# Attention's first tiles: V of batch 0 asked for behind the first q tile, the gate's load moved into ScalarE's program, tile 0's products ahead of the turns of tile 1's q

## The chip, the cores and the metric

The kernel runs on one core of one Trainium2 chip. Its time is the device time of one launch in microseconds (us). Before the change three runs took 647.5, 648.42 and 651.75 us; the median is 648.42 us.

## The reference

The program chains three layers. Only the first is touched by the change, but everything later depends on it.

```
# q, k, v: 4 batches x 8 heads x 576 rows x 64
k_p = k.reshape(B, H, 72, 8, D).mean(axis=3)        # keys pooled by eight
v_p = v.reshape(B, H, 72, 8, D).mean(axis=3)        # values pooled by eight
attn = softmax(q @ k_p.T / sqrt(D));  out = attn @ v_p
x = out.transpose(0, 2, 1, 3).reshape(2304, 512)
logits = x @ w_gate                                  # 8 experts, the best one per token
x = gate_weight * (relu(x @ w1[expert]) @ w2[expert])   # with a capacity per expert
h = x @ w_in;  g = s * relu(h)**2 + b;  y = g @ w_out
```

## The kernel before, in words

Attention is cut into 20 tiles: four batches b, and in each five blocks of 128 rows (the fifth has 64). `load_k`, `load_v` and `load_q` (lines 124 to 137 and 207 to 212) ask for K, V and q from HBM; all of these DMAs stand in the queue of SyncE (SP), in program order, so a load that waits holds back all that follow. K of a batch comes in two DMAs of 576 KB, V in six (576 KB, 448 KB and four of 32 KB), q of a tile in one of 256 KB. K is in pieces of 2 KB, V too, q in pieces of 256 bytes. `load_gate` (lines 116 to 121) asks for the gate's weights `wg` in five small DMAs, and these stand in the program of ScalarE (ACT).

The DMAs of SP and ACT share eight completion counters, named DMAHW0 to DMAHW7 in the order below, which are handed out in turn. A DMA that gets a counter waits until the DMA that had it before has landed. So every load waits for the one eight places ahead of it, whichever queue that was in. Apart from that, a load waits until its buffer is free: q has four buffers, `vraw` has one.

For one tile the work is: `turn_q` transposes q on TensorE (PE) and ACT copies it to `qT` (lines 214 to 222); `products` multiplies it with the pooled keys `kbd` (line 230); `maxima` and `weights` take the row maximum and the difference on VectorE (DVE, lines 236 and 242) and the exponentials on ACT (lines 246 and 247); `turn_e` transposes the exponentials on PE and ACT copies them (lines 259 to 266); `values` multiplies them with `vx` (lines 275 and 277), and DVE divides. `vx` holds the pooled values and, beside them, the pooled values times the gate's weights. `pool_all` sums eight rows to one in three steps, split between DVE and GpSimd (POOL); `prep_v0` turns the pooled values on PE (line 186), copies them and fills `vx`; `prep_v1` multiplies them with `wg` on PE (line 200) and needs all five gate DMAs.

Each engine works in program order. The order of the first tiles is written out by hand, ahead of the loop over the tiles (lines 444 to 482); the change is there. PSUM has one buffer for each of the names `tq`, `te`, `sc`, `o` and `misc`.

Of the kernel before, what the change touches and what calls it, by code (L numbers as in the profile page):

```python
# [72 lines left out]
def rows(t):  # L73
    return P if t < NB - 1 else S - (NB - 1) * P


def attention(nc, tc, c, a, cap, capp, left, big, xd, run, hist, first, ps0):
# [3 lines left out]
    with ExitStack() as es:  # L81
# [34 lines left out]
        def load_gate():  # L116
            wv = a["moe_w_gate"].rearrange("(c q w d) e -> c q d w e", c=2, q=2, w=2)
            for i in range(4):
                ci, q = divmod(i, 2)
                nc.scalar.dma_start(out=wg[D * q:D * q + D, ci, 2 * q:2 * q + 2], in_=wv[ci, q])  # L120
            nc.scalar.dma_start(out=wg[D:P, 2], in_=a["moe_w_gate"].rearrange("(p w d) e -> w d p e", w=2, d=D)[1])
# [3 lines left out]
        def load_k(b):  # L125
            r = big.tile([SP, H, POOL, D], F32, name="kraw")
            src = a["k"][b].rearrange("h (n j) d -> n h j d", j=POOL)
            for i in range(2):
                nc.sync.dma_start(out=r[:, 4 * i:4 * i + 4], in_=src[:, 4 * i:4 * i + 4])
            raw["k", b] = r  # L130

        def load_v(b):
            src = a["v"][b].rearrange("(p w) (n j) d -> w n p j d", w=2, j=POOL)
            nc.sync.dma_start(out=vraw[0:SP, 0:4], in_=src[0])
            nc.sync.dma_start(out=vraw[SP:P, 0:4], in_=src[1, 0:P - SP])
            for p in range(4):
                nc.sync.dma_start(out=vraw[32 * p + 16:32 * p + 32, 4], in_=src[1, P - SP:, p])
            raw["v", b] = vraw
# [24 lines left out]
        def pool_all(kv, b, h0, h1, eng):  # L163
            for _ in pool_steps(kv, b, h0, h1, eng):
                pass

        def prep_k(b):
            tp = ps0.tile([P, 4, SP], F32, name="misc")
            for p in range(4):
                nc.tensor.transpose(tp[:, p], sums["k", b][:, 2 * p:2 * p + 2].rearrange("n h d -> n (h d)"), c.ident[:SP, :SP])  # L170
            for w in range(2):
                r = slice(D * w, D * w + D)
                dst = kbd[b % 2][r, :, SP * w:SP * w + SP]
                if b:
                    nc.scalar.mul(dst, tp[r], KSCALE)
                else:
                    nc.vector.tensor_scalar(out=dst, in0=tp[r], scalar1=KSCALE, scalar2=None, op0=ALU.mult)
# [19 lines left out]
        def prep_v1(b):  # L197
            tr = ps0.tile([P, G, E], F32, name="misc")
            for p in range(3):
                nc.tensor.matmul(tr[:, 4 * p:4 * p + 4].rearrange("r g e -> r (g e)"), lhsT=vts[b][:, p], rhs=wg[:, p].rearrange("d g e -> d (g e)"), start=True, stop=True)  # L200
            nc.vector.tensor_tensor(out=vx[b % 2][:, :, D + 1:], in0=tr, in1=c.mask.unsqueeze(2).to_broadcast([P, G, E]), op=ALU.mult)
# [5 lines left out]
        def load_q(i):  # L207
            if i < N:
                b, t = tiles[i]
                n = rows(t)  # L210
                qs[i] = two.tile([P, H, D], F32, name="q", bufs=4)
                nc.sync.dma_start(out=qs[i][:n], in_=a["q"][b, :, t * P:t * P + n].rearrange("h s d -> s h d"))

        def turn_q(i, bank="tq"):
            if i < N:
                n = rows(tiles[i][1])
                q = qs.pop(i)
                tq = ps1.tile([P, 2, 4, P], F32, name="te")[:, 0] if bank == "te" else ps0.tile([P, 4, P], F32, name="tq")
                for p in range(4):
                    nc.tensor.transpose(tq[:, p, :n], q[:n, 2 * p:2 * p + 2].rearrange("s h d -> s (h d)"), c.ident[:n, :n])  # L220
                qts[i] = two.tile([P, 4, P], F32, name="qT")
                nc.scalar.copy(qts[i][:, :, :n], tq[:, :, :n])

        def products(i, bank="sc"):
            b, t = tiles[i]
            n = rows(t)
            q = qts.pop(i)
            sc = ps1.tile([P, 2, 512], F32, name=bank)
            for p in range(4):
                nc.tensor.matmul(sc[:n, p // 2, p % 2 * 144:p % 2 * 144 + 144], lhsT=q[:, p, :n], rhs=kbd[b % 2][:, p], start=True, stop=True)  # L230
            return sc

        def maxima(i, sc):
            n = rows(tiles[i][1])
            mx = two.tile([P, 2, 4], F32, name="mx")
            nc.vector.tensor_reduce(out=mx[:n], in_=sc[:n, :, 0:288].rearrange("s j (h k) -> s j h k", k=SP), axis=AX.X, op=ALU.max)
            return mx

        def weights(i, sc, mx):
            n = rows(tiles[i][1])  # L240
            s = two.tile([P, 4, 2 * SP], F32, name="s", bufs=3)
            nc.vector.tensor_tensor(out=s[:n].rearrange("s (j p) (w k) -> s j (p w) k", j=2, w=2), in0=sc[:n, :, 0:288].rearrange("s j (h k) -> s j h k", k=SP),
                                    in1=mx[:n].unsqueeze(3).to_broadcast([n, 2, 4, SP]), op=ALU.subtract)

            e = two.tile([P, 4, 32], F32, name="e", bufs=3)
            nc.scalar.activation(e[:n], s[:n, :, 2 * SP - 32:], AF.Exp)
            nc.scalar.activation(s[:n, :, 0:P], s[:n, :, 0:P], AF.Exp)
            ss[i] = s, e
# [8 lines left out]
        def turn_e(i):  # L257
            if i < N:
                n = rows(tiles[i][1])
                s, e = ss.pop(i)  # L260
                te = ps1.tile([P, 2, 4, P], F32, name="te").rearrange("k j p s -> k (j p) s")
                for p in range(4):
                    nc.tensor.transpose(te[:, p, :n], s[:n, p, 0:P], c.ident[:n, :n])
                nc.tensor.transpose(te[:, 4, :n], e[:n].rearrange("s p k -> s (p k)"), c.ident[:n, :n])
                ets[i] = two.tile([P, NB, P], F32, name="eT", bufs=4)
                nc.scalar.copy(ets[i][:, :, :n], te[:, 0:NB, :n])
# [175 lines left out]
                nc.vector.tensor_copy(lists, n)  # L442

        load_k(0)
        load_gate()
        load_q(0)
        load_q(1)
        load_v(0)
        load_q(2)
        load_q(3)  # L450
        load_k(1)
# [6 lines left out]
        o = ps1.tile([P, 2, 512], F32, name="o")  # L458
# [1 line left out]
            nc.tensor.transpose(o[:, 0, 0:P], c.ident, c.ident)  # L460
        turn_q(0)
        prep_k(0)
        turn_q(1, "te")
        sc = products(0, "o"), products(1)
        pool_all("v", 0, 0, 2, nc.gpsimd)
        weights(0, sc[0], maxima(0, sc[0]))
        pool_all("v", 0, 2, NB, nc.vector)
        mx = maxima(1, sc[1])
        turn_e(0)
        prep_v0(0)  # L470
        turn_q(2)
        weights(1, sc[1], mx)
        prep_v1(0)
        turn_q(3)
        scores(2)
# [68 lines left out]
        while todo or tails or scales:  # L544
            more = 7
            while more and (todo or tails):
                more -= 1
                if step():
# [4 lines left out]
                    o = ps1.tile([P, 2, 512], F32, name="o")  # L553
# [1094 lines left out]
```

## Time and profile before

| what | value |
|---|---|
| median of three runs | 648.42 us |
| the profiled execution | 649.79 us |
| its span, first to last instruction | 648.1 us |
| PE busy in the span | 588.7 us (91%) |
| DVE, POOL, ACT busy | 367.0, 267.8, 249.9 us |
| mean granted TensorE clock | 0.959 of 2.4 GHz |

The difference of 1.7 us between the profiled execution and its span lies around the program. The profiled execution is 1.4 us above the median, and inside the three runs shown. A row of the timeline gives the start, the duration and, in brackets, how long the engine had been idle and what ended that. The queue rows (SPq, ACTq) show how long the queue was occupied by issuing a DMA, not the transfer itself.

### The profile page before, as it was taken

How to read it: one execution, taken by the hardware profiler on the slowest of the kernel's cores; microseconds unless marked ns; L12 is line 12 of the kernel's file. 1: busy time of each engine (PE TensorE's matmuls, PEld its weight loads, DVE VectorE, ACT ScalarE, POOL GpSimd, SP SyncE). 2: the span in 40 equal slices, each digit the busy share in tenths (PEclk: the TensorE clock that was granted, in tenths of full speed). 3: DMA queues.
4: the chain of work that ended last, by engine and by line, in shares of the span. 5: the costliest groups of instructions: out<-in, count | busy, mean ns of one | idle time of the engine just before them, and what ended most of it. 6: DMA issues, size and time to landing. Idle time of an engine off the chain costs nothing. (4 is left out here: it accounts for less than half of the span.)

```text
span 648.1 us, 11186 instructions
## 1 busy us (share of the span) xinstructions
PE 588.7 (91%) x4005; PEld 545.1 (84%) x4005; DVE 367.0 (57%) x893; ACT 249.9 (39%) x614; POOL 267.8 (41%) x384
## 2 busy tenths in 40 slices
PE   5887988799899979998887899999999999999894
PEld 5787877689799969997887889899899898898784
DVE  4687898888969956654499996424122021120140
ACT  1354554546356635533327425125034042141130
POOL 6557634627165717013234402216435054153381
PEclk8799999799899979999998799999999999999898
DMA  8999776637649884856565101135200101000000
GB/s 164 190 190 182 157 228 182 220 117 261 230 148 307 267 299 126 281 172 214 188 208 231 34 30 37 32 118 209 81 18 6 46 17 33 32 3 17 20 2 20
DMA packets 67950, 86.11 MB, mean 133 GB/s; under 512 B 24713, under 2 KB 40073, under 8 KB 67856
## 3 DMA queue, kind: packets, MB, share of 16 engines
q1 hardware_dynamic: 57168, 71.04, 37.2%
q10 hardware_dynamic: 8240, 7.14, 3.8%
q0 software_dynamic: 2448, 6.82, 3.3%
q8 instruction: 42, 0.69, 0.5%
q14 instruction: 52, 0.43, 0.2%
HBM read 68.09 MB, written 17.58 MB: 132 GB/s over the span
## 5 line engine op out<-in xcount | busy, mean ns | idle before, releaser
L1440 POOL TENSOR_TENSOR gl<-rt,gh 128x256 fp32r<-128x256 f32 (+1 forms) x96 | 71.3, 747 | 99.3 <-ACT gh L1439 57.9
L1445 PE MATMUL bank<-wo,gh 128*128 128x512 f32 (+1 forms) x340 | 99.2, 376 | 0.0
L1113 PE MATMUL bank<-hs,w2h 128*128 128x288 f32 (+1 forms) x308 | 68.9, 312 | 5.0 <-issue 4.6
L936 POOL TENSOR_TENSOR w1l<-kraw,w1h 128x128 fp32r<-128x128 f32 x96 | 51.9, 572 | 51.1 <-ACT w1h L929 51.1
L1445 PEld LDWEIGHTS bank<-wo,gh 128*128 128x128 f32 x340 | 62.0, 188 | 12.2
L1445 PE MATMUL bank<-wo,gl 128*128 128x512 f32 (+1 forms) x170 | 63.8, 375 | 0.0
L1452 DVE SCALAR_TENSOR_TENSOR raw<-bank,sb,c_u 128x512 f32<-128x512 f32 (+1 forms) x14 | 9.9, 710 | 86.9 <-PE bank L1445 86.9
L1113 PEld LDWEIGHTS bank<-hs,w2h 128*128 128x128 f32 x308 | 51.0, 193 | 6.0 <-issue 5.4
L1424 ACT ACTIVATE rt<-tq 128x256 f32<-128x256 f32 (+1 forms) x26 | 9.5, 367 | 113.8 <-PE tq L1040 91.1
L1113 PE MATMUL bank<-hs,w2l 128*128 128x288 f32 (+1 forms) x148 | 45.0, 304 | 0.0
L1425 DVE SCALAR_TENSOR_TENSOR rt<-bank,rt 128x256 f32<-128x256 f32 (+1 forms) x53 | 21.3, 401 | 37.6 <-ACT rt L1424 37.2
L944 POOL DMA_INDIRECT xg<-xd,u_idx x23 | 26.1, 1136 | 34.4 <-DVE r L290 15.3
L1439 ACT CAST gh<-rt 128x256 fp32r<-128x256 f32 (+1 forms) x96 | 36.6, 381 | 7.9 <-DVE rt L1425 7.9
L1453 POOL DMA_INDIRECT out_dram<-raw,it x12 | 11.9, 994 | 64.3 <-DVE raw L1452 63.8
L1445 PEld LDWEIGHTS bank<-wo,gl 128*128 128x128 f32 x170 | 31.9, 188 | 6.5
L1424 ACT ACTIVATE rt<-bank 128x256 f32<-128x256 f32 (+1 forms) x60 | 22.2, 369 | 33.7 <-PE bank L1040 26.5
L230 PE MATMUL sc<-kbd,qT 128*128 128x144 f32 (+1 forms) x152 | 25.5, 317 | 6.2 <-DVE rmine L380 3.6
L1425 DVE SCALAR_TENSOR_TENSOR rt<-tq,rt 128x256 f32<-128x256 f32 (+1 forms) x24 | 9.6, 399 | 35.5 <-ACT rt L1424 35.5
L967 PE MATMUL bank<-xs,w1h 128*128 128x288 f32 (+1 forms) x120 | 27.3, 313 | 2.0 <-DVE hs L970 2.0
L230 PEld LDWEIGHTS sc<-kbd,qT 128*128 128x128 f32 (+1 forms) x152 | 21.9, 201 | 8.4 <-issue 4.9
L1113 PEld LDWEIGHTS bank<-hs,w2l 128*128 128x128 f32 x148 | 28.5, 193 | 0.0
L940 DVE TENSOR_TENSOR w2l<-vraw,w2h 128x512 fp32r<-128x512 f32 x39 | 26.8, 686 | 0.9 <-ACT w2h L939 0.5
(496 smaller groups left out, 1749.4 us busy)
## 6 DMA issues: line engine op xcount, KB each, us to landing
kraw<-in_moe_w_dram SPq DMA_DIRECT2D x14, 1024.0 KB
vraw<-in_moe_w_dram SPq DMA_DIRECT2D x14, 1024.0 KB
c_raw<-in_moe_w_in_dram ACTq DMA_DIRECT2D x13, 512.0 KB
wo<-in_moe_w_out_dram SPq DMA_DIRECT2D x13, 512.0 KB
kraw<-in_k_dram SPq DMA_DIRECT2D x8, 576.0 KB
out_dram<-c_u SPq DMA_DIRECT2D x1, 4608.0 KB
q<-in_q_dram SPq DMA_DIRECT2D x16, 256.0 KB
xd<-xr SPq DMA_DIRECT2D x16, 256.0 KB
```

Source lines behind the costliest of these rows:

```text
L230: nc.tensor.matmul(sc[:n, p // 2, p % 2 * 144:p % 2 * 144 + 144], lhsT=q[:, p, :n], rhs=kbd[b % 2][:, p], start=True, stop=True)
L936: eng.tensor_sub(self.w1l[:, i, z], self.w1(i)[:, z], self.w1h[:, i, z])
L940: eng.tensor_sub(self.w2l[i], self.w2r[:, i], self.w2h[i])
L944: self.nc.gpsimd.indirect_dma_start(out=dst, out_offset=None, in_=self.xd[:have], in_offset=bass.IndirectOffsetOnAxis(ap=idx[:n], axis=0), ...
L967: self.nc.tensor.matmul(p, lhsT=l[:, f, k], rhs=r[k], start=n == 0, stop=n == 3 * KD - 1)
L1113: nc.tensor.matmul(py[d][:, :v.n], lhsT=l[f][:, d * P:d * P + P], rhs=r[f], start=f == 0 and i == 0, stop=f == KF - 1 and i == 2)
L1424: nc.scalar.activation(r, p, AF.Relu)
L1425: nc.vector.scalar_tensor_tensor(out=p if inside else r, in0=p, scalar=0.0, in1=r, op0=ALU.max, op1=ALU.mult)
L1439: nc.scalar.copy(h[:, :n], r)
L1440: (nc.gpsimd if p is None else nc.vector).tensor_sub(l[:, :n], r, h[:, :n])
L1445: nc.tensor.matmul(p[:, c], lhsT=g[:, j * P:j * P + P], rhs=wo[f][:, z, c], start=f == 0 and i == 0, stop=f == KF2 - 1 and i == 2)
L1453: i = nc.gpsimd.indirect_dma_start(out=dst, out_offset=bass.IndirectOffsetOnAxis(ap=ids, axis=0), in_=o[:, c], in_offset=None, bounds_chec ...
```

## The change

Three things are moved in the hand-written start. V of batch 0 is asked for directly behind q of tile 0, ahead of q of tile 1. `load_gate` is called behind the exponentials of tile 0 instead of ahead of everything. And q of tile 1 is turned after the products of tile 0, in the bank `tq` instead of `te`; the products of tile 1 follow it. Nothing is computed differently.

```
         load_k(0)
-        load_gate()
         load_q(0)
+        load_v(0)
         load_q(1)
-        load_v(0)
         load_q(2)
...
         turn_q(0)
         prep_k(0)
-        turn_q(1, "te")
-        sc = products(0, "o"), products(1)
+        sc = products(0, "o")
         pool_all("v", 0, 0, 2, nc.gpsimd)
-        weights(0, sc[0], maxima(0, sc[0]))
+        weights(0, sc, maxima(0, sc))
+        load_gate()
+        turn_q(1)
+        sc = products(1)
         pool_all("v", 0, 2, NB, nc.vector)
-        mx = maxima(1, sc[1])
+        mx = maxima(1, sc)
         turn_e(0)
         prep_v0(0)
         turn_q(2)
-        weights(1, sc[1], mx)
+        weights(1, sc, mx)
```

On ACT the place is its very start. Before, the five gate DMAs are its first instructions:

```order
L120 DMA wg<-in_moe_w_gate_dram 64x2x8 x4
L121 DMA wg<-in_moe_w_gate_dram 64x4x8
L222 ACT_TABLE_LOAD
L222 COPY qT<-tq 128x512
L222 COPY qT<-te 128x512
L246 ACTIVATE e<-s 128x128
L247 ACTIVATE s<-s 128x4x128
L266 COPY eT<-te 128x640
```

And now:

```order
L222 ACT_TABLE_LOAD
L222 COPY qT<-tq 128x512
L246 ACTIVATE e<-s 128x128
L247 ACTIVATE s<-s 128x4x128
L120 DMA wg<-in_moe_w_gate_dram 64x2x8 x4
L121 DMA wg<-in_moe_w_gate_dram 64x4x8
L222 COPY qT<-tq 128x512
L266 COPY eT<-te 128x640
```

The five issues now stand between the exponentials of tile 0 and the copies of tile 1's q and of tile 0's weights. On PE the place is the stretch from the first turn of q to the turn of tile 3's q. Before:

```order
L220 MATMUL tq<-ident,q 128x128 x4
L170 MATMUL misc<-ident,kp 128x72 x4
L220 MATMUL te<-ident,q 128x128 x4
L230 MATMUL o<-kbd_163,qT 128x144 x4
L230 MATMUL sc<-kbd_163,qT 128x144 x4
L263 MATMUL te<-ident,s 128x128 x4
L264 MATMUL te<-ident,e 128x128
L186 MATMUL misc<-ident,vp 128x128 x3
```

And now, from the products of tile 0 on, with the counters that PE waits for:

```order
L230 MATMUL o<-kbd_163,qT 128x144 [waits DVE_49,Activation_49]
L230 MATMUL o<-kbd_163,qT 128x144 x3
L220 MATMUL tq<-ident,q 128x128 [waits DMAHW1_49,PE_49]
L220 MATMUL tq<-ident,q 128x128 x3
L230 MATMUL sc<-kbd_163,qT 128x144 [waits Activation_49]
L230 MATMUL sc<-kbd_163,qT 128x144 x3
L263 MATMUL te<-ident,s 128x128 [waits DVE_49]
...
L200 MATMUL misc<-wg,vT 128x32 [waits DMAHW4_49,DMAHW3_49,DVE_49]
L200 MATMUL misc<-wg,vT 128x32 [waits DMAHW6_49,DMAHW5_49]
L200 MATMUL misc<-wg,vT 128x32 [waits DMAHW0_49]
L220 MATMUL tq<-ident,q 128x128 [waits DMAHW7_49,Activation_49]
```

The turn of tile 1's q and its products now stand between the products of tile 0 and everything that is made of V, and the gate's five counters are 3, 4, 5, 6 and 0. On SP the place is the queue of loads. Before, the loads behind V of batch 0 wait for counters of K, V and q:

```order
L129 DMA kraw<-in_k_dram 72x4x512 [waits DMAHW1_49,DVE_49,Pool_49]
L129 DMA kraw<-in_k_dram 72x4x512 [waits DMAHW2_49]
L457 DMA idc<-big_ids 96x30 [waits DMAHW3_49]
L212 DMA q<-in_q_dram 64x8x64 [waits DMAHW4_49,PE_49]
L212 DMA q<-in_q_dram 128x8x64 [waits DMAHW5_49,PE_49]
L212 DMA q<-in_q_dram 128x8x64 [waits DMAHW7_49,DMAHW6_49,PE_49]
L212 DMA q<-in_q_dram 128x8x64 [waits DMAHW0_49,PE_49]
L134 DMA vraw<-in_v_dram 72x4x512 [waits DVE_49,Pool_49]
```

And now:

```order
L129 DMA kraw<-in_k_dram 72x4x512 [waits DMAHW1_49,DVE_49,Pool_49]
L129 DMA kraw<-in_k_dram 72x4x512 [waits DMAHW2_49]
L456 DMA idc<-big_ids 96x30 [waits DMAHW3_49]
L212 DMA q<-in_q_dram 64x8x64 [waits DMAHW4_49,PE_49]
L212 DMA q<-in_q_dram 128x8x64 [waits DMAHW5_49,PE_49]
L212 DMA q<-in_q_dram 128x8x64 [waits DMAHW6_49,PE_49]
L212 DMA q<-in_q_dram 128x8x64 [waits DMAHW7_49,PE_49]
L134 DMA vraw<-in_v_dram 72x4x512 [waits DMAHW0_49,DVE_49,Pool_49]
```

The rows read nearly alike, but before the change the gate had the counters 2 to 6 at the very start and V of batch 0 had them next; now the gate has 3, 4, 5, 6 and 0 directly ahead of these rows. So the loads of `idc`, of q of tiles 4, 5 and 6, and of V of batch 1 now wait for a gate DMA each.

## Rows read from the trace of the kernel before

**Rows 1.** The page: two engines' busy time, and the DMA in 40 slices.

```profile
PE 588.7 (91%) x4005; PEld 545.1 (84%) x4005; DVE 367.0 (57%) x893; ACT 249.9 (39%) x614; POOL 267.8 (41%) x384
DMA  8999776637649884856565101135200101000000
```

**Rows 2.** Windows: stretch, length, busy PE, PEld, DVE, ACT, POOL; clock; DMA share; GB/s.

```profile
20.00:30.00 10.00, 7.75 (x42) 7.28 (x41) 6.24 (x10) 3.71 (x7) 6.27 (x9) 0.66 1.00 194
30.00:40.00 10.00, 8.70 (x71) 7.87 (x70) 8.03 (x18) 5.83 (x13) 3.94 (x6) 1.00 1.03 186
40.00:50.00 10.00, 9.52 (x78) 8.92 (x77) 8.96 (x21) 5.86 (x14) 8.35 (x13) 1.00 0.92 206
50.00:60.00 10.00, 9.50 (x81) 8.39 (x78) 5.67 (x21) 4.70 (x11) 7.05 (x11) 1.00 0.94 176
60.00:100.00 40.00, 33.75 (x263) 30.38 (x262) 36.88 (x121) 23.05 (x48) 20.28 (x27) 0.96 0.73 181
```

**Rows 3.** Timeline of DVE: its waits for K and V.

```profile
10.66 0.95 DVE L154 TENSOR_TENSOR kraw<-kraw 72x768 f32<-72x768 f32 x1 [0.69 <-DMA kraw<-in_k_dram]
20.39 1.03 DVE L154 TENSOR_TENSOR vraw<-vraw 128x768 f32<-128x768 f32 x1 [1.68 <-DMA vraw<-in_v_dram]
40.46 0.83 DVE L154 TENSOR_TENSOR vraw<-vraw 128x512 f32<-128x512 f32 x1 [1.88 <-DMA vraw<-in_v_dram]
59.98 0.54 DVE L154 TENSOR_TENSOR vraw<-vraw 128x256 f32<-128x256 f32 x1 [3.03 <-DMA vraw<-in_v_dram]
```

**Rows 4.** Timeline of ACT and its queue: the gate's issues and tile 0.

```profile
1.14 2.93 ACTq L120 DMA_DIRECT2D wg<-in_moe_w_gate_dram  x4
4.10 0.63 ACTq L121 DMA_DIRECT2D wg<-in_moe_w_gate_dram  x1
12.96 0.58 ACT L222 COPY qT<-tq 128x512 f32<-128x512 f32 x1 [6.91 <-PE tq L220]
19.08 0.63 ACT L247 ACTIVATE s<-s 128x512 f32<-128x512 f32 x1
```

**Rows 5.** Timeline of PE, from the turn of tile 1's q on.

```profile
13.55 1.06 PE L220 MATMUL te<-ident,q 128*128 128x128 f32 x4
16.91 1.88 PE L230 MATMUL sc<-kbd,qT 128*128 128x144 f32 x8
22.79 0.90 PE L186 MATMUL misc<-ident,vp 128*128 128x128 f32 x3 [2.25 <-POOL vp L160]
24.34 1.49 PE L200 MATMUL misc<-wg,vT 128*128 128x32 f32 x6
25.65 1.09 PE L220 MATMUL tq<-ident,q 128*128 128x128 f32 x4
26.53 2.13 PE L230 MATMUL sc<-kbd,qT 128*128 128x144 f32 x8
28.45 1.26 PE L275 MATMUL o<-vx,eT 128*128 128x146 f32 x8
31.08 1.25 PE L230 MATMUL sc<-kbd,qT 128*128 128x144 f32 x8
```

**Rows 6.** DMA packets by queue (q1 SP, q10 ACT): 0:45, 10.5:11, 11:11.5.

```profile
q10 hardware_dynamic: 848, 0.02, 1.6%
q10 hardware_dynamic: 138, 0.00, 16.3%
q1 hardware_dynamic: 377, 0.10, 103.4%
```

**Rows 7.** Timeline of SP's queue: K, q of tile 7, V of batches 1 and 2.

```profile
0.82 0.85 SPq L129 DMA_DIRECT2D kraw<-in_k_dram  x2
26.77 2.28 SPq L212 DMA_DIRECT2D q<-in_q_dram  x1
29.14 0.95 SPq L134 DMA_DIRECT2D vraw<-in_v_dram  x1
45.01 2.68 SPq L134 DMA_DIRECT2D vraw<-in_v_dram  x1
```

## The prediction

> **What bounds the kernel now.** I read the page first: PE is busy 91% of the span and the DMA is nearly full in the first slices only [rows 1]. The change sits in the first 30 us, so the question is which resource there decides when the rest can start. The windows by stage answer that. From 20 to 60 us the DMA share is 0.92 to 1.03, while no engine is full; from 60 to 100 us DVE is, with 36.88 of 40 us, and the DMA falls to 0.73 [rows 2]. So attention runs in two parts: up to 60 us on the transfers, then on DVE. The timeline of DVE shows the joints: it stood idle for V of batch 0 (1.68 us, until 20.39), of batch 1 (1.88 us, until 40.46) and of batch 2 (3.03 us, until 59.98) [rows 3]. Work on DVE that comes late by less than such a wait costs nothing behind it, and work that comes early gains nothing. Behind the last of them DVE has hardly a gap, so I take a shift at 59.98 to the end in full.
>
> **The change, part by part.** The sum is made against the profiled execution (649.79 us); the median is 1.4 us lower, and I put the sum on the median, 648.4.
>
> The gate leaves the head. Its 848 packets took 1.6% of the first 45 us, 0.72 us of all DMA engines [rows 6]. Without them K's second half, which landed at 10.66 [rows 3], lands 0 to 0.7 us earlier; I take 0.4, since most of its packets lay beside K. The products of tile 0 and its exponentials move with it: they ended at 19.08 + 0.63 = 19.7 [rows 4], now at 19.3.
>
> V comes ahead of q of tile 1. V of batch 0 then lands earlier by about the time of one q, 256 KB at 185 to 195 GB/s, an estimate of 1.4 us. That buys nothing where it is used: its pooled form is turned on PE, and PE now has the turn and the products of tile 1 ahead of that. In return q of tile 1 lands last of the same pieces, at about 20.4, when V did [rows 3]. Its turn (1.06 us [rows 5]) is over by 21.5. That would be the path, but ACT hides it.
>
> ACT issues the gate. The five issues ran from 1.14 to 4.73, 3.6 us [rows 4]; they now stand between the exponentials and the copy of tile 1's q. ACT is free at 19.3 + 3.6 = 22.9. Bounds: SP's issues at the start took 0.42 each, 2.1 for five [rows 7]; the gate's own row is the nearest, so 3.6. The trace differs here from the Trainium skill, "DMA: Bandwidth & Descriptors", "Issuing engines are not separate DMA queues", which calls the sequencer's time to start a DMA usually small relative to the DMA: these five cost ACT five times the DMA time that they fill. By the page this term is nearly nothing and the time some 649; it is weighed as a rival.
>
> PE behind it. Copy 0.58 [rows 4], a handover, products 1.88 [rows 5]: 25.6. Five turns of tile 0's exponentials at the pace of the 1.06 us row (four of them), 1.3: 26.9. So V's turns start at 26.9 instead of 22.79, **4.1 us late**. V's lead is gone.
>
> The gate's arrival. `prep_v1` came 1.55 us behind V's turns [rows 5]; it would be ready at 28.4, if the gate is there. Before, the last issue ended at 4.73, and the last gate packets passed between 10.5 and 11.0; after 11.0 the whole load is on q1 [rows 6]. That is 6.3 us of delay behind K, whose pieces of 2 KB filled SP's queue. K of batch 1 fills it now in the same way. The same lag gives 22.9 + 6.3 = 29.2; the lower bound is no wait at all (28.4), the upper 30.5, with a landing of about a microsecond on top. I take 29.2, the same kind of neighbours. From there to the end of tile 3's turn took 2.4 us (24.34 to 26.74) [rows 5]. Around there the clock rises: the granted clock is 0.66 in the mean of 20 to 30 us and 1.00 from 30 on [rows 2], and the products that took 2.13 us before the rise took 1.25 behind it [rows 5]. I give half a microsecond of that to the turn, which ends at 31.1 (4.4 late), and the rest to the products, so that the values of tile 0 start at 32.3 instead of 28.45, **3.8 us late**. PE had 1.3 us idle from 30 to 40 [rows 2], so between 2.5 and 3.8 of it reach DVE; I take 3.8: DVE is ready for V of batch 1 at 40.46 - 1.88 + 3.8 = 42.4.
>
> SP behind that. q of tile 7 waits for the turn of tile 3's q: it was issued at 26.77, the moment the turn ended, and the issue took 2.28 us because the queue was full [rows 7]. Now it stands at 31.1, and V of batch 1 behind it at about 31.6 instead of 29.14, +2.5. Not all of that shows in the landing, since before V had to wait its turn among packets already queued. If the DMA never runs dry, V is late only by the gate's 0.7 us, at 41.2; if all shows, 43.0. The middle is 42.1. DVE's 42.4 is behind it, so DVE takes V of batch 1 at 42.4, **+1.9**.
>
> To the last joint. V of batch 2 was issued at 45.01, right behind the pooling of batch 1, and its first DMA took 2.68 us to issue [rows 7]: the queue was full, and the DMA share stays at 0.92 and 0.94 [rows 2]. So the stream keeps its shift of about 1.8, with 0.5 as the lower end (the 1.4 us that the shares leave free in those 20 us made up). DVE's own lateness of 1.9 fits into its 3.03 us. Hence V of batch 2 at 61.8, and **+1.8 at the end: 650.2 us**. Its own bounds, +0.5 to +2.5 with the scatter of half a microsecond to one, are 648.3 to 651.6.
>
> Costed at nothing: the earlier pooling of V (PE is late), the bank `tq` instead of `te` (free when its turn comes, by the copy of tile 0's q at 13.54 [rows 4]), and the other counters of the first loads (V is now asked for well ahead of the end of q of tile 0, so SP has more work queued, not less).
>
> **The rivals.** First, **the gate is cheap**: issues at 0.42 us, and the packets pass without waiting for K. ACT is free at 21.4, V's turns start at 25.4, `prep_v1` runs at 26.9, tile 3's turn ends at 29.3, and the values start 2 us late. That is absorbed by DVE's 1.88, and V of batch 1 is late by the DMA's 0.7 only: 648.4 + 0.5 = 648.9. Against it stands the row of 3.6 us. The page's rule leads here too. Chance 0.24.
>
> Second, **the start gains**: not slower, though I forecast slower. If the transfers alone decide, all that counts is what lies ahead of V of batch 2 in the queue; the gate's 0.72 us then find room where the share is below one, from 40 to 60 us [rows 2], and K's 0.4 to 0.7 us reach 59.98: 647.8. It decides if V of batch 1 is not late, so only if SP reaches it by about 29. For it speaks that the stream, not PE, ended the idle time at all three joints; against it that SP's place there waits for a turn on PE. Chance 0.09.
>
> Third, **SP is held by the gate**. The loads of `idc` and of q of tiles 4, 5 and 6 wait for one gate DMA each (the order's counters 3 to 6). Before, the first of these q's left at about 20.4, when V had landed [rows 3]. If the gate's DMAs pass only behind K of batch 1 altogether, at 30 us and later, SP has nothing under way when K ends, the DMA runs dry for about 3 us, and the q's of tiles 4 to 7 (128 KB and three of 256 KB, 4.7 us at 190 GB/s) still lie ahead of V of batch 1. It lands 0.7 + 3 us and a little more late, at about 44.4: +3.9, 652.3. It decides if the gate lands later than about 29.5. The long lag of the gate before speaks for it; that the 6.3 us of the row lead to 29.2, just short of that point, speaks against it. Chance 0.17.
>
> **How the numbers follow.** The forecast has 0.47, the three rivals 0.24, 0.09 and 0.17; 0.03 stays for a loss that I don't see, such as a clock that stays low longer. The range from 647.8 to 652.8 takes in the forecast with its bounds, the cheap gate, most of the third and part of the second. One per cent, 6.5 us, is about what a measurement of this kernel can tell from no change, and no case with a mechanism reaches it: faster by over 1% 0.02, within 1% 0.94, slower by over 1% 0.04.
>
> **What the changed kernel's profile would show.** The five ACTq rows behind tile 0's exponentials, 0.6 to 0.9 us each, and the copy of tile 1's q directly behind them. V's turns on PE near 27. Line 200 waiting for the DMA of `wg`, about a microsecond. SP's q of tile 7 near 31. DVE's wait for V of batch 1 nearly gone and ending near 42.4, that for batch 2 ending near 61.8. I am wrong if ACT issues the gate in 2 us, if line 200 does not wait or waits over 2 us, or if the wait for batch 2 ends before 60.5 or after 63.

## The result and the profile after

The changed kernel is **slower by 1.1%**: 657.5 us (median of four runs, 654.05 to 660.06) against 648.89 us for the kernel before beside it (four runs), ratio 1.0112 with a 95% interval of 1.0076 to 1.0148. Run again beside 17 more runs of before it took 655.76 us, ratio 1.0104 (1.0056 to 1.0152). The forecast was 650.2 us, its range ended at 652.8, and slower by over 1% had a chance of 0.04. The profiled execution took 658.09 us with a span of 656.4 us, 8.3 us more than that of before.

Up to 60 us the trace reads nearly as forecast. The page, against [rows 1]: PE's busy time is 3 us more, and the DMA has a dent in its second slice.

```profile
PE 591.7 (90%) x4005; PEld 548.2 (84%) x4005; DVE 369.2 (56%) x893; ACT 249.9 (38%) x614; POOL 266.1 (41%) x384
DMA  8799676636649893854487102116200101000000
```

The windows by stage, to be set against [rows 2] (columns as there):

```profile
20.00:30.00 10.00, 6.08 (x34) 5.38 (x33) 4.65 (x8) 3.50 (x7) 6.06 (x9) 0.67 0.70 157
30.00:40.00 10.00, 9.66 (x69) 9.31 (x69) 7.03 (x15) 3.35 (x8) 1.93 (x4) 0.85 1.05 207
50.00:60.00 10.00, 9.96 (x79) 8.87 (x79) 7.98 (x27) 7.21 (x17) 7.32 (x11) 1.00 0.94 190
60.00:100.00 40.00, 32.48 (x245) 29.18 (x245) 33.42 (x107) 19.80 (x42) 21.24 (x29) 0.91 0.72 174
```

From 20 to 30 us the DMA share is 0.70, where it was 1.00. SP tells why. Its queue, against [rows 7]:

```profile
25.67 0.35 SPq L456 DMA_DIRECT2D idc<-big_ids  x1
27.76 3.04 SPq L212 DMA_DIRECT2D q<-in_q_dram  x4
30.90 0.84 SPq L134 DMA_DIRECT2D vraw<-in_v_dram  x1
```

The waits of that queue from 15 to 33 us (what waited for what, us in total, times, longest):

```profile
SPq L456 <- DMA wg<-in_moe_w_gate_dram: 5.3, 1, 5.3
SPq L212 <- DMA wg<-in_moe_w_gate_dram: 1.7, 1, 1.7
```

`idc` and the q's behind it stood for the gate's DMAs, since they get the gate's counters; V of batch 1 left 1.8 us later than before. On ACT, against [rows 4], the gate's issues run from 18.98 to 22.42, and the copy of tile 1's q follows them:

```profile
18.98 2.78 ACTq L120 DMA_DIRECT2D wg<-in_moe_w_gate_dram  x4
21.80 0.62 ACTq L121 DMA_DIRECT2D wg<-in_moe_w_gate_dram  x1
22.46 0.58 ACT L222 COPY qT<-tq 128x512 f32<-128x512 f32 x1 [2.85 <-DMA wg<-in_moe_w_gate_dram]
```

On PE, against [rows 5], V's turns are late and `prep_v1` (line 200) waits twice for `wg`:

```profile
26.25 0.49 PE L186 MATMUL misc<-ident,vp 128*128 128x128 f32 x3
27.84 0.38 PE L200 MATMUL misc<-wg,vT 128*128 128x32 f32 x2 [0.65 <-DMA wg<-in_moe_w_gate_dram]
28.82 0.60 PE L200 MATMUL misc<-wg,vT 128*128 128x32 f32 x4 [0.60 <-DMA wg<-in_moe_w_gate_dram]
31.71 1.83 PE L275 MATMUL o<-vx,eT 128*128 128x146 f32 x8
```

DVE takes V of batch 1 at 42.12 without a wait, and V of batch 2 at 61.15, so the joint of [rows 3] is 1.17 us late (forecast 1.8):

```profile
42.12 0.83 DVE L154 TENSOR_TENSOR vraw<-vraw 128x512 f32<-128x512 f32 x1
61.15 0.60 DVE L154 TENSOR_TENSOR vraw<-vraw 128x256 f32<-128x256 f32 x1 [1.62 <-DMA vraw<-in_v_dram]
```

The other 7 us come behind that joint, in code that the change does not touch, and in two places. **The first is at 70 to 78 us.** The timelines of PE and DVE after:

```profile
71.46 2.26 PE L230 MATMUL sc<-kbd,qT 128*128 128x144 f32 x8 [2.44 <-DVE r L288]
73.52 2.15 PE L275 MATMUL o<-vx,eT 128*128 128x146 f32 x8
78.17 0.25 DVE L442 COPY u_lists<-o 48x96 f32<-48x96 f32 x1 [2.86 <-PE o L437]
```

The same copy on DVE in the kernel before:

```profile
73.77 0.25 DVE L442 COPY u_lists<-o 48x96 f32<-48x96 f32 x1 [0.34 <-PE o L437]
```

Behind the wait of 2.44 us the products take 2.26 us, nearly twice the 1.22 us that they took before at full clock, and DVE waits for them. The copy is 4.40 us late, 3.2 more than the joint. The windows of 4 us there show the granted clock (the third number from the end) between its two levels, 1.2 and 2.4 GHz; before it was 1.00 in both. The kernel before had its own low spell earlier (0.78 from 60 to 65 us and 0.88 from 65 to 70 us, where it is 1.00 after), so the 3.2 us are what is left between the two:

```profile
70.00:74.00 4.00, 2.54 (x10) 2.57 (x11) 3.71 (x9) 2.62 (x7) 3.92 (x6) 0.58 0.05 11
74.00:78.00 4.00, 4.00 (x21) 3.52 (x20) 1.28 (x2) 1.84 (x5) 2.25 (x4) 0.57 0.65 177
```

**The second is at 300 to 313 us**, in the expert layer: four groups of eight matmuls on `vraw` and then one of 32. PE before, from the first group to the group of 32:

```profile
296.08 1.22 PE L1248 MATMUL bank<-rt,vraw 128*128 128x144 f32 x8 [2.24 <-ACT w1h L1089]
297.50 1.12 PE L1248 MATMUL bank<-rt,vraw 128*128 128x144 f32 x7
298.87 0.28 PE L1248 MATMUL bank<-rt,vraw 128*128 128x144 f32 x1 [0.25 <-issue]
...
302.30 4.19 PE L1248 MATMUL bank<-hs,vraw 128*128 128x144 f32 x32
```

and after (the same line is L1249 there):

```profile
300.65 1.22 PE L1249 MATMUL bank<-rt,vraw 128*128 128x144 f32 x8 [2.18 <-ACT w1h L1090]
...
302.08 1.00 PE L1249 MATMUL bank<-rt,vraw 128*128 128x144 f32 x6
305.92 0.46 PE L1249 MATMUL bank<-rt,vraw 128*128 128x144 f32 x2 [2.84 <-issue]
...
309.38 2.29 PE L1249 MATMUL bank<-rt,vraw 128*128 128x144 f32 x8
312.02 4.63 PE L1249 MATMUL bank<-hs,vraw 128*128 128x144 f32 x32
```

From the first group to the group of 32 it was 6.22 us before and is 11.37 us after: 5.15 us lost. PE stops in the middle of a group, at a matmul that waits for nothing in the program ("issue"), for 2.84 us, and then runs at half clock (granted 0.61 from 305 to 310 us). Of the total some 1.4 us is won back by the end. So the 8.3 us are 1.2 at the joint, 3.2 by the clock at 70 us, 5.15 at 300 us, less 1.4.

What PE stops for is read from one of the two DMA queues that the page calls "instruction", q8: 42 packets, 0.69 MB, so 16 KB each. The packets of that queue and of SP's (count, MB, share) before, from 296 to 298 us:

```profile
q1 hardware_dynamic: 123, 0.25, 46.5%
q8 instruction: 1, 0.02, 4.2%
```

and in the second run of the changed kernel, where PE ran dry at 299.39 us, PE and the packets from 299 to 301 us:

```profile
298.39 1.00 PE L1249 MATMUL bank<-rt,vraw 128*128 128x144 f32 x6
302.19 0.49 PE L1249 MATMUL bank<-rt,vraw 128*128 128x144 f32 x2 [2.79 <-issue]
q1 hardware_dynamic: 386, 0.76, 100.4%
q8 instruction: 1, 0.02, 3.1%
```

Before, a piece of 16 KB passes at 296.19 us, while the DMA still has room, and PE goes on at 298.87 us, 2.7 us later. After, it passes at 299.65 us, when PE has run dry and the DMA is full of expert weights, and PE goes on at 302.19 us, 2.5 us later. I call these pieces PE's code pages. That they are PE's rests on the experiments, which move the stop by moving PE's program.

### The profile page after: what moved, and what is told of

It reads as the page before. It is cut to its first block, busy times and chain, and to the rows that moved or that the text cites. A ratio compares the mean times of both kernels' runs of the same rounds, so it can differ in the third digit from the quotient of the medians.

```text
span 656.4 us, 11187 instructions
## 1 busy us (share of the span) xinstructions
PE 591.7 (90%) x4005; PEld 548.2 (84%) x4005; DVE 369.2 (56%) x893; ACT 249.9 (38%) x614; POOL 266.1 (41%) x384
```

## The experiments

The experiments came in four groups, each beside its own runs of the kernel before, whose medians were 650.63 (31 runs), 650.84 (17), 651.65 (19) and 650.75 us (35). The table has what the reading rests on. "V2" is when DVE takes V of batch 2. "Split" is how many matmuls stand ahead of and behind the stop in its group of eight, with the idle time; "groups" is the time from the first group of eight to the group of 32, both from PE's timeline.

| kernel | median, us | ratio to before (95%) | V2 | split, idle us | groups, us |
|---|---|---|---|---|---|
| before | | | 59.98 | 7 + 1, 0.25 | 6.22 |
| before, once more | 651.17 | one run | 59.58 | 7 + 1, 2.45 | 10.00 |
| changed | 657.5 | 1.0112 (1.0076 to 1.0148) | 61.15 | 6 + 2, 2.84 | 11.37 |
| changed, again | 655.76 | 1.0104 (1.0056 to 1.0152) | 61.11 | 6 + 2, 2.79 | 11.36 |
| gate moved only | 653.43 | 1.0030 (0.9998 to 1.0063) | 62.87 | 7 + 1, 0.77 | 6.73 |
| V ahead only | 652.71 | 1.0004 (0.9968 to 1.0039) | 61.62 | none | 7.35 |
| products' order only | 654.31 | 1.0045 (1.0018 to 1.0072) | 59.66 | 6 + 2, 2.40 | 11.78 |
| changed, gate at start | 654.99 | 1.0063 (1.0033 to 1.0093) | 60.69 | 6 + 2, 2.24 | 9.69 |
| changed, 2 idle transposes fewer | 657.35 | 1.0095 (1.0048 to 1.0141) | 62.49 | none | 9.10 |
| the same, once more | 653.43 | one run | 61.98 | none | 8.83 |
| before, 2 idle transposes more | 655.74 | 1.0100 (1.0066 to 1.0134) | 58.43 | 5 + 3, 3.37 | 11.97 |
| changed, PE kept busy at 70 us | 658.13 | 1.0142 (1.0093 to 1.0190) | 62.77 | first group, 5 + 3, 4.38 | 12.22 |
| before, page far | 650.65 | 0.9977 (0.9946 to 1.0008) | 59.38 | none | 5.78 |
| before, page far, again | 649.89 | 0.9988 (0.9964 to 1.0011) | 58.48 | none | 5.77 |
| changed, page far | 653.84 | 1.0029 (1.0001 to 1.0057) | 63.13 | none | 5.78 |
| gate only, page far | 652.52 | 1.0034 (1.0012 to 1.0056) | 62.46 | none | 5.78 |
| products' order only, page far | 649.21 | 0.9983 (0.9958 to 1.0008) | 58.57 | none | 5.77 |
| gate at start, page far | 650.40 | 0.9999 (0.9975 to 1.0022) | 58.89 | none | 5.78 |

**First, one part at a time.** Two theories: the granted clock and a stop far behind the start make the loss, whichever part is done; or the gate alone makes it.

The gate moved alone, in the kernel before:

```
-        load_gate()
         load_q(0)
...
         weights(0, sc[0], maxima(0, sc[0]))
+        load_gate()
```

> Of the three moves only the gate's: its five loads stand behind the exponentials of tile 0, V and the products stay where they were. Theory of the clock: the whole change made V of batch 2 come only 1.2 us later (61.15 instead of 59.98), and the rest of the 8 us came from PE's granted clock and a stall behind 60 us; then a single move that delays that joint by about a microsecond gives 648 to 655 us, as the clock falls. Theory of the gate: the loss comes from the gate alone (the issues of 3.6 us on ACT and SP waiting for its counters); then this kernel loses nearly all of the 8 us, 655 to 658, and the two others nothing. In the profile: line 200 waits for the gate near 27 us, and the values of tile 0 start 1 to 3 us later than 28.45.

V of batch 0 ahead of q of tile 1, alone:

```
         load_q(0)
+        load_v(0)
         load_q(1)
-        load_v(0)
```

> Only V of batch 0 is asked for ahead of q of tile 1; tile 1's q is still turned ahead of the products of tile 0. PE then waits for that q, which lands near 19 us, before it can do the products of tile 0: these move from 14.86 to about 20.5, and the values of tile 0 from 28.45 to some 32. Theory of the gate: no loss at the end, 648 to 650, since the joints at 40.46 and 59.98 absorb it. Theory of the clock: V of batch 2 within 1.5 us of before, and 649 to 656 by where the granted clock falls behind it.

The order of the products, alone:

```
-        turn_q(1, "te")
-        sc = products(0, "o"), products(1)
+        sc = products(0, "o")
...
+        turn_q(1)
+        sc = products(1)
```

> Only PE's order is changed: tile 1's q is turned after the exponentials of tile 0 in program order, the loads stay where they were. That q has landed at 13.4 at the latest, so PE turns it behind the products of tile 0; the products of tile 1 end near 21 instead of 18.8, and V's turns at 22.79 hardly move. Both theories: 647 to 650 us. If it loses more than 3 us, the lateness at the start is not what decides.

The whole change, with the gate left at the start:

```
         load_k(0)
+        load_gate()
         load_q(0)
...
         weights(0, sc, maxima(0, sc))
-        load_gate()
```

> The changed kernel with the gate's loads back at the very start. ACT is free for the copy of tile 1's q once it is turned (near 20.5), so V's turns start near 24 instead of 26.2, line 200 waits for nothing, and V of batch 2 lands within 0.5 us of 59.98. Theory of the gate: 648 to 650. Theory of the clock: between 648 and 656, by whether PE's granted clock falls near 70 us and near 306 us as in the changed kernel; the time follows the low stretches in the profile, about half of their length each, and not the lateness at 60 us.

No part alone brings the loss, and the two kernels with the new order of the products but without the gate's move lose 0.45 and 0.63%, though both theories gave the first of them 647 to 650 us (it took 654.31) and the theory of the gate gave the second 648 to 650 (654.99). So the gate alone is not the cause. But the theory of the clock allowed everything between 648 and 656 and is not confirmed by that either. What showed the way was a pattern in the table: every kernel with the new order of the products stops at 6 + 2 for over 2 us; the kernels without it stand at 7 + 1 or show no stop. In the new order PE's program has two wait instructions more, 100 against 98 in the trace (the expectation below says one; the turn of tile 1's q now also waits for PE's own work in the bank `tq`). So all that follows stands two instructions, one matmul with its weight load, later in PE's program, and the border between two pieces of code falls one matmul earlier.

**Second, the code page.** The changed kernel again, no edit:

> The changed kernel once more, beside more runs of the kernel before. Theory of the code page: in all three kernels with the new order of the products (the change itself and the two experiments that keep that order) PE's program has one wait more, its page boundary falls one matmul earlier in the first products behind 300 us, and PE stands there 2.2 to 2.8 us for its own code, with a spell of low granted clock behind it; in the three without that order it stands 0.25 us at most. It expects the stall here again and a median of 654 to 657.5, about 1.0% over before. Theory of chance (the scatter of before is several us, the first comparison had few runs): a median of 651 to 654, no stall at 300 us in this profile.

The stop came again (2.79 us), 655.76 us. In this execution the clock at 70 to 78 us stayed at 1.00, and DVE's wait for the lists was 0.45 us; the copy was 1.60 us late. What else it lost came at 300 us, where the groups took 11.36 us. So the low clock at 70 us is not a fixed part of the loss, while the stop came both times.

Two idle transposes fewer at the start of the changed kernel:

```
-        for _ in range(33):
+        for _ in range(31):
             nc.tensor.transpose(o[:, 0, 0:P], c.ident, c.ident)
```

> The changed kernel with 31 instead of 33 of the idle transposes at the very start, which PE does long before the first q lands. Nothing else differs, so PE's program is four instructions shorter ahead of 300 us. Theory of the code page: the boundary falls back to where it was, the stall of 2.84 us at 305.9 goes (0.5 us at most is left), the low clock of 306 to 313 us with it, and the time is 4 us under the changed kernel of the same call, about 651 to 653; what is left over before, 1 to 3 us, is the start and the clock at 70 to 77 us. Rival, the stall comes from the DMA being full of weight loads at that time, whatever the code's place: stall of 2 us or more stays, time within 1 us of the changed kernel.

The kernel before with two more, so `range(35)` instead of `range(33)`:

> The kernel before with 35 instead of 33 of the idle transposes at the start; PE's program is four instructions longer ahead of 300 us, and attention is untouched. Theory of the code page: PE stalls 2 to 3 us in the products at about 300 us, the clock falls behind it, and the time is 3 to 5 us over before: 653 to 656. Rival, the stall belongs to the changed start: no stall, time within 1 us of before.

PE of the kernel before with two transposes more, at 300 us:

```profile
293.12 1.22 PE L1248 MATMUL bank<-rt,vraw 128*128 128x144 f32 x8 [2.00 <-ACT w1h L1089]
...
294.54 0.88 PE L1248 MATMUL bank<-rt,vraw 128*128 128x144 f32 x5
298.78 0.66 PE L1248 MATMUL bank<-rt,vraw 128*128 128x144 f32 x3 [3.37 <-issue]
...
305.09 4.55 PE L1248 MATMUL bank<-hs,vraw 128*128 128x144 f32 x32
```

Two transposes, done 290 us earlier in PE's wait for the first q, make the kernel before slower by 1.0%, as much as the change, and the stop is two matmuls earlier in its group than before. Its attention is not late at all (V of batch 2 at 58.43). The other direction was a miss: with two fewer the visible stop went, but the groups still took 9.10 us, since the clock fell there all the same, and the median, 657.35 us, is no better; the runs lie in two lots, 651 to 656 and 659 to 663 us.

PE kept busy in its wait at 70 us:

```
+            if i == 8:
+                idle = ps0.tile([P, 4, P], F32, name="tq")
+                for _ in range(14):
+                    nc.tensor.transpose(idle[:, 0], c.ident, c.ident)
             turn_q(i + 4)
```

> The changed kernel with 14 idle transposes more in attention, in PE's wait of 2.44 us ahead of the products at 71.5 us. Theory of the clock: the granted clock stays at 1.00 from 70 to 78 us, the products take 1.2 us instead of 2.26, DVE's wait of 2.86 us for the lists at 78 is under 0.5, and PE is 3 us earlier at 80 us than in the changed kernel; these transposes also move PE's code by some 29 instructions, so the stall at 306 may go or come elsewhere and is read apart from it: 654 with the stall, 650 without. Rival, the lateness of 4.4 us at 78 comes from DVE's own work: at 80 us no gain over the changed kernel.

The granted clock was 1.00 from 70 to 78 us, the products took 1.15 us, and DVE's wait for the lists was 1.03 us. The copy came at 77.03, against 78.17. From V of batch 2 to the copy it took 14.26 us, where the first run of the changed kernel took 17.02; but its second run took the same 14.26 us without these transposes, so this run does not show that they kept the clock up. The forecast of 3 us missed by size: V of batch 2 was itself 1.6 us later than in the changed kernel, and a spell of low clock came at 65 to 70 us (0.66). The 14 transposes moved the stop eleven matmuls ahead, to 4.38 us, and the whole was slower still.

**Third, the page far away.** 22 small transposes behind the 33 move the border ahead of PE's wait for ACT, into a stretch where the DMA carries almost nothing:

```
+        for _ in range(22):
+            nc.tensor.transpose(o[:64, 0, 0:64], c.ident[:64, :64], c.ident[:64, :64])
```

In the kernel before:

> The kernel before with 22 idle transposes of 64x64 more behind the 33 at the start, in PE's wait for the first q; they put the boundary of PE's code page at 300 us some 22 matmuls earlier, ahead of PE's wait for ACT at 294 to 296 us, where the DMA share is under 0.1. Theory of the code page: no stall for code between 296 and 303 us (0.25 us or less), no low clock there, time within 1.5 us of before: 649 to 652. Rival, any longer program of PE costs (the two transposes more cost 1.0%, so these cost as much or more whatever the place): 655 or more.

In the changed kernel:

> The changed kernel with the same 22 idle transposes of 64x64 more at the start. Theory of the code page: the stall of 2.8 us behind 300 us is gone and the clock stays at 1.00 there; PE is later than before by 1.2 to 1.8 us at 60 us and by no more than that (and, if the clock falls at 70 us, 3 us more) at 320 us: 651 to 654, 3 to 5 us under the changed kernel. Rival, the loss is the changed start's alone, by lateness that grows: 655 to 658 though no stall is seen.

Two single executions beside them, without new edits (the first is the kernel with 31 transposes, the second the kernel before):

> The changed kernel with 31 idle transposes at the start once more, one look: its runs lay at 651 to 653 or at 659 to 663 in nearly equal number. Theory of the code page: with the boundary at the edge, the stall at 300 us comes in some executions and not in others; a run at 659 or more shows it, a run at 653 or less does not. Rival, the slower runs lose elsewhere: the stall is absent though the run is at 659.

> The kernel before once more, one look, for the scatter of its trace. Theory of the code page: no stall for code above 0.5 us between 296 and 303 us, whatever the time (646 to 654). Theory of chance: a stall of 2 us or more there.

PE of the changed kernel with the page far:

```profile
300.15 1.22 PE L1251 MATMUL bank<-rt,vraw 128*128 128x144 f32 x8 [2.06 <-ACT w1h L1092]
...
301.57 1.25 PE L1251 MATMUL bank<-rt,vraw 128*128 128x144 f32 x8
...
305.93 4.19 PE L1251 MATMUL bank<-hs,vraw 128*128 128x144 f32 x32
```

and of the kernel before in its second execution:

```profile
295.13 1.12 PE L1248 MATMUL bank<-rt,vraw 128*128 128x144 f32 x7
298.71 0.28 PE L1248 MATMUL bank<-rt,vraw 128*128 128x144 f32 x1 [2.45 <-issue]
...
303.71 4.19 PE L1248 MATMUL bank<-hs,vraw 128*128 128x144 f32 x32
```

This settles the second place. With the page far there is no stop there, the clock stays at 1.00 (5.78 us for the groups), and the changed kernel loses 0.29% instead of 1.04 to 1.12%. 55 transposes at the start don't cost where 35 did, so it is the place and not the length. The forecast for the kernel before missed: I expected no stop, and there was one of 2.45 us in a run of 651.17 us. The kernel before stands on the edge and stops in some executions. The execution with 31 transposes fell into the lower lot (653.43 us, no stop), so what its upper lot loses was not seen.

A count in the traces says the same more directly. In all nine executions that stop in the groups, from 0.25 to 4.38 us, the first matmul behind the stop has 3823 of PE's instructions ahead of it (once 3824), whichever matmul of the groups that is. So the place belongs to PE's program and not to the data. PE goes on there 2.5 to 3.2 us behind the start of its 16 KB piece, and in the three executions without a stop and with the border in the groups it comes to that count 2.5 to 3.4 us behind the piece. So the length of a stop goes with how late the piece passes. That goes with the DMA: in the microsecond ahead of the piece its share was 1.03 to 1.14 in the seven executions that stopped for 2.2 us or more, and 0.00 to 0.25 in the five others.

With the page far, that count falls a few matmuls ahead of the wait for ACT, in a microsecond with a DMA share of 0.00 to 0.07, and PE does not stop in any of six executions. The move is not free of charge, though: five of the six have a new stop of 0.69 to 1.39 us in the next group of 32 matmuls on `rt`, near 320 us.

**Fourth, which part is left.** The parts again, all with the 22 small transposes: the gate alone, the products' order alone, the change with the gate at the start, and the kernel before.

> Kernel before with the gate asked for behind the exponentials of tile 0, V and the products as before, and the 22 idle transposes of 64x64 at the start. Theory of the held SP: the gate alone makes SP wait (idc and q of tile 4 leave at 25 us or later, not at 20), the DMA share of 20 to 30 us falls under 0.9, V of batch 2 is 1 to 3 us late, and the time is 2 to 3.5 us over the kernel before with the same transposes: 652 to 654. Rival, the order of the products makes the loss: within 1 us of that kernel.

> Kernel before with the order of the products alone and the 22 idle transposes. Theory of the code page and the held SP: no stall at 300 us, V of batch 2 within 0.5 us of before, time within 1 us of the kernel before with the same transposes: 649.5 to 652 (with the page in its old place the same order lost 0.45%). Rival, the order costs by itself: 653 or more.

> The whole change but the gate, which is asked for at the start as before, and the 22 idle transposes. Theory of the code page and the held SP: SP issues idc and q of tile 4 at about 20 us, V of batch 2 is late by 1 us at most, time within 1.2 us of the kernel before with the same transposes: 650 to 652.5 (0.63% over before with the page in its old place). Rival, V ahead of q and the order make the loss: 653 or more.

> The kernel before with the 22 idle transposes again, five rounds. Theory of the code page: the kernel before stands on the edge of the page (no stall in one look, 2.45 us in another), so with the page moved far the mean gains 1 to 2 us: ratio 0.997 to 0.999, no run over 653. Rival, the transposes change nothing: ratio 1.000.

Now the parts come apart. The products' order costs nothing (649.21 us, and 649.89 us for the kernel before beside it); V ahead of q and the order together cost half a microsecond by the medians (650.40), which the intervals don't tell from nothing. The gate alone costs 2.6 us. In those kernels, SP's queue with the gate moved alone:

```profile
22.28 10.09 SPq L212 DMA_DIRECT2D q<-in_q_dram  x4
32.47 0.49 SPq L134 DMA_DIRECT2D vraw<-in_v_dram  x1
```

and in the change with the gate at the start:

```profile
20.53 8.94 SPq L212 DMA_DIRECT2D q<-in_q_dram  x4
29.57 0.97 SPq L134 DMA_DIRECT2D vraw<-in_v_dram  x1
```

V of batch 1 leaves 2.9 us later. With the gate alone `idc` left at 21.83 us, not at 25 as I had expected; the q's behind it stood instead, 5.9 us in three waits for the gate's DMAs, and the DMA share of 20 to 30 us was 0.86. The last of SP's waits ahead of V was another, that of tile 7's q for PE's turn of tile 3's q, which ended at 31.98 us:

```profile
SPq L212 <- DMA wg<-in_moe_w_gate_dram: 5.9, 3, 3.7
SPq L212 <- PE tq L220: 2.1, 1, 2.1
```

So the gate's move delays V by two ways, through the counters and through PE, and no run separates them. The kernel before with the page far is the best lead for a version that beats both, with the products' order alone beside it: 0.9977, 0.9988 and 0.9983, each with an interval that still holds 1. None is shown to beat the kernel before.

## Why the prediction was wrong

The step that failed is the last of the bottleneck reading: **"Behind the last of them DVE has hardly a gap, so I take a shift at 59.98 to the end in full"**, and with it the end of the sum, "+1.8 at the end". The shift arrived; what I added up stopped there, and behind it the profiled execution lost 3.2 us more by the clock at 70 us and 5.15 us by PE's stop for its code at 300 us, of which it won back 1.4. The three signs that would have shown me wrong (ACT's issues in 2 us, line 200 waiting not at all or over 2 us, V of batch 2 before 60.5 or after 63) all stayed away, since each of them lies ahead of that joint and most of the loss behind it.

- **The gate's issues on ACT** were right: 3.44 us against 3.6, ACT free at 22.4 against 22.9. On the Trainium skill, "DMA: Bandwidth & Descriptors", "Issuing engines are not separate DMA queues": the sequencer's time that it calls usually small was again nearly five times the 0.72 us of DMA that these issues fill, so the measurement decides.
- **V's turns on PE** came at 26.25 against 26.9, **the gate's arrival** held `prep_v1` 1.25 us against 0.8, and **the values of tile 0** started at 31.71 against 32.3. The steps are right within 0.7 us.
- **V of batch 1 without a wait** at 42.12 against 42.4, right. **V of batch 2** at 61.15 against 61.8, inside its bounds. Over the ten executions with the gate at the start V of batch 2 was taken at 59.5 us in the mean, over the eight with it moved at 62.2: +2.7 us where the sum has 1.8. The term has the right sign and is small by a third.
- **The route of that term** was a mixture of the forecast and the third rival, SP held by the gate. V of batch 1 left by the forecast's route: the turn of tile 3's q, forecast to end at 31.1, let tile 7's q go at 30.0 us, and V followed at 30.9. But the queue of loads was not kept full ahead of that: SP stood 5.3 us for the gate and the DMA share fell to 0.70. The rival's 3.9 us were too many for the profiled run, but the changed kernel with the page far, with V of batch 2 at 63.13 against 59.38 for the kernel before with the page far, came close to them.
- **"up to 60 us on the transfers, then on DVE"** was read from windows that end at 100 us and is no bound of what lies behind: PE and its code pages set the pace at 300 us. The sum had no term for an instruction more on PE. Its price is read from the runs: the groups at 300 us took 11.4 us in the changed kernel, 6.2 or 10.0 before, and 5.8 when the page is far.
- **The 0.03 "for a loss that I don't see, such as a clock that stays low longer"** is where the result fell. That was far too little: the trace of before had low spells behind PE's waits, and "issue" stops of PE of 4.57 us at 235 us and 1.65 us at 316 us, and I had not looked that far back. (All eighteen traces have a stop at each of these two places, always ahead of the same matmul, so they are not the stop that moved; what they are for stays open.)
- **The anchor** was low as well. I put the sum on 648.4, the median of three runs; the medians of 17 to 35 runs were 650.6 to 651.7. That the kernel before stops in some executions too may be a part of that; its medians with the page far, 649.89 and 650.65, don't show how much. From 650.8 the same +1.8 leads to 652.6, against 653.84 for the changed kernel with the page far.

So of the loss about 3 us are the gate's (3.2 us between the two kernels with the page far, 2.6 us for the gate alone), and the rest is the place of the code page: 0.75 to 0.83% between the ratios of the changed kernel with the page in its place and far away, 1.9 to 3.7 us between their medians, 5.6 us in the groups of the executions seen. From this goes what the page takes of the kernel before, 0.12 to 0.23% by ratios whose intervals still hold 1. Both parts are shown; how much the page takes on average is known no better than that. Why the page was asked for ahead of the weights at 7 + 1 in one execution and behind them in another, and what the upper lot of the runs with 31 transposes loses, stays open.

## What to carry to other kernels

An edit changes the program's length as well as its order: when the loss lies far behind the edited place, look at the long "issue" waits of the changed trace, and move the program by a few idle instructions to see whether the loss moves with them. Compare single parts only with that place held fixed, or the parts will not add up. And a small load moved to another queue can hold the main queue through the shared completion counters, though its bytes are next to nothing.

## What the runs showed of the hardware

- PE stopped 0.25 to 4.4 us at one count of its instructions, 2.2 us or more where the 16 KB piece passed with the DMA full of weights (share of 1.03 to 1.14 just ahead of it), 0.77 us or less where it passed with a share of 0.25 or less, and not at all in the six executions where that count fell into a microsecond with a DMA share of 0.07 or less. Two transposes, 290 us earlier, moved the stop by two matmuls and the time by 1.0%.
- A stop cost 1.5 to 2.5 times its length where it was 2.2 us or more, with half clock behind it: 2.79 us idle became 5.6 us (11.36 against 5.78 us for the groups). The clock also fell there without any stop: with 31 transposes the groups took 8.83 and 9.10 us.
- In attention a wait of PE of 2.44 us was followed by half clock (0.58 from 70 to 74 us); in another execution of the same kernel the wait at that place was 2.07 us and the clock stayed at 1.00. The clock fell to 0.57 to 0.81 in a part of 70 to 78 us in three of the eight executions with the gate moved, and in one of the ten others, to 0.85. So 3 us there come and go from run to run.
